# A decode kernel's five engine programs: emitted inside a block, or directly behind the common opening

## The chip, the cores and the metric

The kernel runs on one core of a Trainium2 chip. The metric is the device time of one execution in microseconds (us), lower being better. The core has five engines, each with a program of its own: PE (TensorE, matmuls), DVE (VectorE), ACT (ScalarE), POOL (GpSimd) and SP (SyncE, which here only issues transfers and waits for them). They meet through semaphores. Transfers run on 16 DMA engines.

## The reference

One decode step of a transformer block for a batch of 8 with one token each: sliding-window attention over cached keys and values, then a small MLP, each behind a layer norm.

```python
# x: 8 x 1 x 512; caches: 8 x 8 x 8192 x 128 bf16; 32 query heads, 8 kv heads
def _A_ref(x, k_cache, v_cache, wq, wo):
    W = min(4096, max(256, Sk // 4))              # 2048
    q = (x @ wq).reshape(B, Sq, Hq, Dh)           # transposed to b h q d
    k = repeat(k_cache[:, :, Sk - W:, :], rep)    # the last 2048 positions
    v = repeat(v_cache[:, :, Sk - W:, :], rep)
    scores = einsum("bhqd,bhkd->bhqk", q, k) * (Dh ** -0.5)
    p = softmax(scores)
    o = einsum("bhqk,bhkd->bhqd", p, v)
    return o.reshape(B, Sq, Hq * Dh) @ wo

def _B_ref(x, w1, w2, w3, w4):
    ...                                           # token shifts are all zero for S == 1
    x1 = x + hs
    return x1 + gelu(layernorm(x1) @ w3) @ w4

h  = x + _A_ref(layernorm(x), ...)
h2 = h + _B_ref(layernorm(h), ...)
```

## The kernel before

The kernel reads some 79 MB: for each of the 64 pairs of batch row and kv head 512 KB of keys and 512 KB of values, and the weights. SP issues all of these transfers on one queue (the helper `dma`, L181): first `wq`, then keys four heads at a time (`load_k`), values head by head (`load_v`), the slices of `wo` in between, and at the end `w3` and `w4`. PE transposes the keys (L277), ACT and DVE evict them (L285, L287), PE forms the scores (L299), the softmax runs per batch row in five steps, and the values are multiplied in (L359, L375). Behind the last pair come the output projection, the second layer norm and the MLP. The last steps are an addition on DVE (L598), a transposition on PE (L601), a copy to `out_sb` on DVE (L602), and SP's transfer of the 8 KB output (L605), behind which SP waits for `sem_out` in the function `store`.

The order on each engine is written out by hand. An object `Engine` collects the operations of one engine with the semaphore values that each waits for; nothing is emitted while they are collected. `Engine.emit` then writes the list to an engine: a wait where one is needed, the instruction, and an increment of the engine's own semaphore behind it. The kernel's last lines call `emit` for the five engines.

Ahead of all of this stands a common opening that the framework puts in when the program object is made (L628): POOL fills four constants, every engine drains, and the engines meet. Four engines report to POOL through one semaphore, and POOL releases them through another.

In the kernel before, the five calls of `emit` stand inside a `Block` (L609 to L614). A block gives each engine a section of its own. An unconditional branch leads each engine from the opening to its section, and another from the end of its section to a common end; at the end each engine drains, and the engines meet once more in the same way as in the opening. On SP the wait for `sem_out`, which has no instruction of its own behind it, rides on the branch to the end.

Of the kernel before, what the change touches and what calls it, by code (L numbers as in the profile page):

```python
# [67 lines left out]
def bass_sequential_preLN__sliding_block_cached__mixer_s_mlp__decode_kernel(  # L68
# [23 lines left out]
    with es:  # L92
# [84 lines left out]
        PE, AC, DV, PO, SP = (Engine(S(n)) for n in ("s_pe", "s_act", "s_dve", "s_pool", "s_sp"))  # L177
# [428 lines left out]
            e.wait_ge(sem_out, 16)  # L606
        SP.op(store, e_out, inc=False)

        with nc.Block() as block:  # L609
            block.gpsimd(PO.emit)  # L610
            block.sync(SP.emit)
            block.tensor(PE.emit)
            block.scalar(AC.emit)
            block.vector(DV.emit)  # L614


# [26 lines left out]
```

## Time and profile before

| | |
|---|---|
| median of three runs | 198.69 us (198.63 to 198.71) |
| span of the profiled execution, first to last instruction shown | 196.8 us |
| the profiled execution's own time | not listed; the median stands for it |
| between span and median | 1.9 us |
| transferred | 79.48 MB, mean 404 GB/s |
| PE, PEld, DVE, ACT, POOL busy | 149.0, 98.1, 83.1, 89.6, 7.7 us |

PE is TensorE's matmuls and PEld its weight loads. A name with a q behind it (SPq, PEq) is the engine's sequencer, which issues transfers and handles branches, drains and semaphores; such instructions are not counted as busy. A releaser, as in "<-DVE out_sb L602", is what ended the idle time before an instruction.

### The profile page before, as it was taken

What the parts mean: (1) busy time and instruction counts of PE and PEld (TensorE: products, weight loads), DVE (VectorE), ACT (ScalarE), POOL (GpSimd) and SP (SyncE); (2) the same over time, 40 slices, a digit from 0 to 9 for tenths busy, and PEclk for the clock granted to TensorE, in tenths of its full rate; (3) what the DMA queues carried; (4) which work ended last, traced back from release to release, by engine and by line L of the source; (5) the groups of instructions that cost most, each with busy time, mean ns of one, the idle gap of its engine ahead of it and who ended that gap; (6) DMA issues with size and microseconds to landing.
All of it is one profiled execution on the core that took longest, in us unless ns stands there. A gap on an engine that the chain in (4) does not pass through costs nothing.

```text
span 196.8 us, 4638 instructions
## 1 busy us (share of the span) xinstructions
PE 149.0 (76%) x2077; PEld 98.1 (50%) x2077; DVE 83.1 (42%) x182; ACT 89.6 (46%) x103; POOL 7.7 (4%) x16
## 2 busy tenths in 40 slices
PE   0037999999982989649992898669796989678854
PEld 0014666666640747237660656356554655235753
DVE  7502645446541346315451255416443544432231
ACT  3003766766751475424761365526652665420330
POOL 8300000000000000000000000000000000000030
PEclk9999999999999699966999699969997999965555
DMA  6999999999999999999999999999999999999991
GB/s 235 453 403 433 426 430 398 422 426 424 402 425 411 441 406 404 437 406 446 395 421 411 439 413 434 417 431 418 435 414 433 414 411 418 417 423 414 411 322 40
DMA packets 18276, 79.48 MB, mean 404 GB/s; under 512 B 1480, under 2 KB 7376, under 8 KB 16080
## 3 DMA queue, kind: packets, MB, share of 16 engines
q1 hardware_dynamic: 18240, 79.18, 98.0%
q8 instruction: 16, 0.26, 0.5%
q14 instruction: 4, 0.03, 0.0%
q10 hardware_dynamic: 16, 0.01, 0.0%
HBM read 79.18 MB, written 0.01 MB: 402 GB/s over the span
## 4 chain that ended last, share of the span: by engine, by line
DMA 70%; PE 22%; SPq 5%; DVE 1%; issue 1%; ACT 0%
DMA knat<-in_A_k_cache_dram 52%; PE kT_ps L277 13%; DMA vnat<-in_A_v_cache_dram 10%; DMA w_sb<-in_B_w_dram 9%; PE S_ps L299 6%; SPq L181 5%; PE o_rows L375 1%; PE o_rows L395 1%; PE sm L336 1%; PE S_ps L593 0%; DVE orow L385 0%; ACT orow L384 0%; PE o_rows L250 0%; PE sm L322 0%; PE sm L348 0%
## 5 line engine op out<-in xcount | busy, mean ns | idle before, releaser
L285 ACT ACTIVATE kT_sb<-kT_ps 128x1024 bf16<-128x1024 bf16 x64 | 65.4, 1024 | 61.2 <-PE kT_ps L277 61.2
L277 PE MATMUL kT_ps<-ident_b,knat 128*128 128x128 bf16 x1024 | 74.3, 231 | 21.8 <-DMA knat<-in_A_k_cache_dram 21.8
L277 PEld LDWEIGHTS kT_ps<-ident_b,knat 128*128 128x128 bf16 x1024 | 63.2, 104 | 46.2 <-DMA knat<-in_A_k_cache_dram 28.0
L287 DVE COPY kT_sb<-kT_ps 128x1024 bf16<-128x1024 bf16 x64 | 44.3, 694 | 59.0 <-PE kT_ps L277 59.0
L299 PE MATMUL S_ps<-kT_sb,qblk 128*32 128x512 bf16 x256 | 40.9, 612 | 0.0
L385 DVE TENSOR_TENSOR orow<-o_rows,orow 128x512 bf16<-128x512 f32 x14 | 9.7, 691 | 25.2 <-ACT orow L384 25.2
L375 PE MATMUL o_rows<-vnat,pT_sb 128*32 128x512 bf16 x224 | 15.6, 399 | 3.7 <-DMA vnat<-in_A_v_cache_dram 2.9
L384 ACT ACTIVATE orow<-o_rows 128x512 bf16<-128x512 f32 x14 | 8.6, 612 | 13.3 <-PE o_rows L375 13.2
L326 ACT ACTIVATE P_sb<-S_ps,negcol 128x512 bf16<-128x512 f32 x8 | 11.3, 1406 | 3.3 <-DVE negcol L325 3.3
L375 PEld LDWEIGHTS o_rows<-vnat,pT_sb 128*32 128x32 bf16 x224 | 6.2, 101 | 11.1 <-issue 8.3
L299 PEld LDWEIGHTS S_ps<-kT_sb,qblk 128*32 128x32 bf16 x256 | 7.2, 93 | 6.0 <-issue 1.2
L233 PE MATMUL S_ps<-wbig,xlnT 128*32 128x512 bf16 x32 | 3.6, 625 | 5.2 <-DMA wbig<-in_A_wq_dram 5.2
L581 POOL TENSOR_SCALAR r<-vsum 128x8 f32<-128x8 f32 x1 | 0.2, 243 | 182.8 <-DVE vsum L565 182.8
L395 PEld LDWEIGHTS o_rows<-sel,orow 128*128 128x128 bf16 x112 | 3.9, 101 | 5.8 <-issue 4.0
L239 ACT ACTIVATE qrow<-S_ps 128x512 bf16<-128x512 f32 x1 | 0.6, 597 | 12.2 <-PE S_ps L233 12.2
L216 PE MATMUL sm<-ident_b,xln_b 8*128 8x8 bf16 x4 | 0.3, 174 | 7.7 <-DVE xln_b L204 7.7
L308 DVE TENSOR_REDUCE mcol<-S_ps 128x1 f32<-128x512 f32 x8 | 5.5, 682 | 0.8 <-PE S_ps L299 0.8
L395 PE MATMUL o_rows<-sel,orow 128*128 128x4 bf16 x112 | 5.1, 167 | 0.6 <-DVE orow L385 0.6
L359 PEld LDWEIGHTS kT_ps<-pT_sb,vnat 128*128 128x128 bf16 x128 | 4.0, 105 | 2.6 <-issue 1.7
L233 PEld LDWEIGHTS S_ps<-wbig,xlnT 128*32 128x32 bf16 x32 | 1.3, 140 | 6.7 <-issue 6.7
L359 PE MATMUL kT_ps<-pT_sb,vnat 128*128 128x4 bf16 x128 | 4.5, 167 | 0.0
L322 PE MATMUL sm<-ones_f,negrow 1*128 1x1 f32 x16 | 3.0, 256 | 1.5 <-DVE negrow L318 1.5
(83 smaller groups left out, 83.6 us busy)
## 6 DMA issues: line engine op xcount, KB each, us to landing
knat<-in_A_k_cache_dram SPq DMA_DIRECT2D x16, 2048.0 KB, 19.4
vnat<-in_A_v_cache_dram SPq DMA_DIRECT2D x64, 512.0 KB, 18.6
wbig<-in_A_wq_dram SPq DMA_DIRECT2D x1, 4096.0 KB, 12.3
wbig<-in_A_wo_dram SPq DMA_DIRECT2D x4, 1024.0 KB, 20.3
w_sb<-in_B_w_dram SPq DMA_DIRECT2D x1, 1792.0 KB, 14.7
w_sb<-in_B_w_dram SPq DMA_DIRECT2D x1, 896.0 KB, 16.6
w_sb<-in_B_w_dram SPq DMA_DIRECT2D x1, 768.0 KB, 16.8
w_sb<-in_B_w_dram SPq DMA_DIRECT2D x1, 128.0 KB, 9.6
```

The source lines that it names most:

```text
L181: e.dma_start(dst, src).then_inc(sem, 16)
L277: ins = e.matmul(kT_ps[i % 2][:, n * 128:(n + 1) * 128], knat[:, i // KQ % NK, r * DH:(r + 1) * DH], ident_b[:, :], is_transpose=True)
L285: e_lo[i] = AC.op(lambda e: e.activation(kT_sb[:, i % NKT, 0:W // 2], kT_ps[i % 2][:, 0:W // 2], ACT.Copy), e_Tlo[i], e_QK.get(i - NKT))
L287: e_hi[i] = DV.op(lambda e: e.tensor_copy(kT_sb[:, i % NKT, W // 2:W], kT_ps[i % 2][:, W // 2:W]), e_Thi[i], e_QK.get(i - NKT))
L299: ins = e.matmul(S_ps[b % 2][32 * t:32 * (t + 1), :], qblk[:, b, g - g % KQ + t, at:at + H], kT_sb[:, i % NKT, :].rearrange("p (n t) -> p ...
L308: e_max[b] = DV.op(lambda e: e.tensor_reduce(mcol[:, :], S_ps[b % 2][:, :], AX.X, ALU.max), e_QK[G * b + G - 1], e_mT.get(b - 1))
L326: e_exp[b] = AC.op(lambda e: e.activation(P_sb[:, j, :].rearrange("p (c a w) -> p c w a", c=4, w=KQ), S_ps[j][:, :].rearrange("p (c w a) - ...
L359: ins = e.matmul(dst, vnat[:, i % NV, c * DH:(c + 1) * DH], pT_sb[:, b % 2, c, hq(g):hq(g) + R], start=(c == 0), stop=(c == NC - 1))
L375: ins = e.matmul(o_rows[32 * u:32 * (u + 1), :], pT_sb[:, b % 2, c, :], vnat[:, v0:v0 + KQ, c * DH:(c + 1) * DH], start=(c < 4), stop=(c > ...
L384: e = AC.op(lambda e: e.activation(orow[:, 0, :], o_rows[:, :], ACT.Copy), e_PV[i], e_oT.get(i - KQ))
L385: e_olo[i] = DV.op(lambda e: e.tensor_tensor(orow[:, 1, :], o_rows[:, :], orow[:, 0, :], ALU.subtract), e)
L395: ins = e.matmul(o_rows[:, R * t:R * (t + 1)], orow[:, part, t * DH:(t + 1) * DH], sel32[:, h:h + R], start=(part == 0), stop=(part == 1), ...
```

## The change

The block is gone. The five `emit` calls write straight behind the opening:

```diff
         SP.op(store, e_out, inc=False)
 
-        with nc.Block() as block:
-            block.gpsimd(PO.emit)
-            block.sync(SP.emit)
-            block.tensor(PE.emit)
-            block.scalar(AC.emit)
-            block.vector(DV.emit)
+        SP.emit(nc.sync)
+        AC.emit(nc.scalar)
+        PO.emit(nc.gpsimd)
+        DV.emit(nc.vector)
+        PE.emit(nc.tensor)
```

Each engine loses its two unconditional branches, its drain at the end and its part in the meeting at the end. On SP the wait for `sem_out` becomes a semaphore instruction of its own, the last of SP's program. The opening with its meeting stays. The operations of each engine, their order and their waits are the same; that the five lists are emitted in another order among themselves does not show, since each engine has its own program.

## The prediction

> **What bounds the kernel now.** I read the page first: the span, the DMA row, the rate and the chain that ended last.
>
> ```profile
> span 196.8 us, 4638 instructions
> DMA  6999999999999999999999999999999999999991
> GB/s 235 453 403 433 426 430 398 422 426 424 402 425 411 441 406 404 437 406 446 395 421 411 439 413 434 417 431 418 435 414 433 414 411 418 417 423 414 411 322 40
> ...
> q14 instruction: 4, 0.03, 0.0%
> ...
> DMA 70%; PE 22%; SPq 5%; DVE 1%; issue 1%; ACT 0%
> ```
>
> From the second slice to the last but one the DMA engines are busy at 9 tenths or more and move some 420 GB/s. The chain lies on DMA for 70% of the span. The body of the kernel, about 189 us of it, is a stream of keys, values and weights. The change touches no instruction of that body: engine by engine the two programs hold the same work in the same order, and only what stands ahead of the body and behind it differs. So I forecast no change between the first transfer and the store, and look at the two ends.
>
> The end first. The timeline of the last microseconds, and then the waits of SP's queue (us in total, times, longest):
>
> ```profile
> 194.12 0.22 DVE L598 TENSOR_TENSOR fT<-fin,S_ps 128x32 bf16<-128x32 f32 x1 [1.42 <-PE S_ps L593]
> 194.73 0.21 DVE L602 COPY out_sb<-sm 32x128 bf16<-32x128 bf16 x1 [0.38 <-PE sm L601]
> 194.97 0.37 SPq L605 DMA_DIRECT2D out_dram<-out_sb  x1
> ```
>
> ```profile
> SPq L605 <- DVE out_sb L602: 9.3, 1, 9.3
> SPq L609 <- DMA out_dram<-out_sb: 1.0, 1, 1.0
> SPq L609 <- PEq L609: 0.2, 1, 0.2
> ```
>
> DVE writes the output rows at 194.73, SP issues the store at 194.97, the issue takes 0.37, SP then waits 1.0 for the data to land, and it waits 0.2 more in something that has the line number of the block, L609. Up to the landing (194.97 + 0.37 + 1.0 = 196.34, about 196.4) everything is needed in the changed kernel too. What follows is the block's end. The view of that line lists all of it (duration ns min/median/max, first and last start):
>
> ```profile
> L609 POOLq EVENT_SEMAPHORE  x2: 17/17/17, 196.6 to 196.7; - x2
> L609 POOLq DRAIN  x1: 1782/1782/1782, 190.5 to 190.5; - x1
> L609 ACTq DRAIN  x1: 957/957/957, 191.3 to 191.3; - x1
> L609 PEldq DRAIN  x1: 342/342/342, 194.4 to 194.4; - x1
> L609 DVEq DRAIN  x1: 251/251/251, 194.7 to 194.7; - x1
> L609 SPq COMPARE_BRANCH  x1: 33/33/33, 196.4 to 196.4; - x1
> L609 SPq DRAIN  x1: 13/13/13, 196.5 to 196.5; - x1
> L609 SPq EVENT_SEMAPHORE  x1: 17/17/17, 196.7 to 196.7; - x1
> L609 ACTq EVENT_SEMAPHORE  x1: 17/17/17, 196.7 to 196.7; - x1
> L609 DVEq EVENT_SEMAPHORE  x1: 21/21/21, 196.7 to 196.7; - x1
> L609 PEldq EVENT_SEMAPHORE  x1: 51/51/51, 196.7 to 196.7; - x1
> ```
>
> Read it as a sequence. SP's branch holds the wait for the store and goes through at 196.4. SP drains at 196.5. POOL, the gatherer, sees the fourth arrival at 196.6 and releases the rest, and all leave at 196.7. Then the span ends, at 196.8. Two window rows show what runs meanwhile (busy us per engine, then granted clock, DMA share, GB/s):
>
> ```profile
> 194.97:196.38 1.41, 0.00 (x0) 0.00 (x0) 0.00 (x0) 0.00 (x0) 0.00 (x0) 0.50 0.03 6
> 196.38:196.80 0.42, 0.00 (x0) 0.00 (x0) 0.00 (x0) 0.00 (x0) 0.00 (x0) 0.50 0.05 20
> ```
>
> No engine computes in either, so the 0.42 us of the second row are bare.
>
> **The change part by part.**
>
> *Front branches.* The program before has one unconditional branch on each engine ahead of its work. The chain's first pieces (start, us) show what SP's costs:
>
> ```profile
> 0.66 0.07 issue
> 0.73 0.41 SPq L181
> 1.14 0.06 issue
> 1.19 16.63 DMA knat<-in_A_k_cache_dram
> ```
>
> Between the opening barrier and SP's first transfer, where the branch stands, lie 0.07 us. Between that transfer and the next, where no branch stands, lie 0.06. The branch is worth 0.01 at most, and no view has an instruction on lines 610 to 614. I take 0, with 0 and 0.01 as ends. The other engines start into waits that end far later than 0.7, so theirs are worth nothing. [...]
>
> *Drains of POOL, ACT, PE and DVE.* They take 1.78, 0.96, 0.34 and 0.25 us, but begin at 190.5, 191.3, 194.4 and 194.7. The last ends by 195.0, and the store's landing at 196.4 covers all of them: 0. Without that cover the longest remaining excess would be DVE's 0.25.
>
> *SP's branch, drain and the end barrier.* The conditional branch becomes a plain wait of the same semaphore as SP's last instruction: 17 ns (SP's EVENT_SEMAPHORE) in place of 33. Nothing of the kernel is queued behind it, and no engine waits for it. The way from the landing to the release then goes. It began at 196.4 (the branch, with 0.03 of its own) and ended with the span at 196.8: by the window row 0.42 us at most, and from it 0.02 for the wait that stays and what the rounded edges add. I take 0.35, from 0.30 to 0.40. This part lowers the span.
>
> *What comes behind the span.* The time is 198.69 us, the median of three runs (198.63 to 198.71), and the span 196.8. The own time of the profiled execution is not listed, so I set the sum against the median and carry the 1.9 us between the two as work without rows. If, as I take it, the engines meet once more in this remainder, then in the kernel before all five go into it together at 196.7, and the meeting ends with the slowest of them. In the changed kernel four of them reach it by 195.0 and only SP comes late. So a second gain is how much later than SP the slowest engine is on such a way. The nearest rows are those at the other end, where the engines come from the runtime's opening into the kernel:
>
> ```profile
> L628 SPq DRAIN  x1: 7/7/7, 0.0 to 0.0; - x1
> L628 DVEq DRAIN  x1: 10/10/10, 0.1 to 0.1; - x1
> L628 ACTq DRAIN  x1: 8/8/8, 0.1 to 0.1; - x1
> ...
> L628 PEldq DRAIN  x1: 8/8/8, 0.3 to 0.3; - x1
> ```
>
> SP is first, at 0.0, and PE last, at 0.3; DVE and ACT come at 0.1. PE's semaphore instruction in the list of L609 is also the slowest, 51 ns against 17. So PE is 0.2 behind the middle two and 0.3 behind SP. If SP's lead is its own speed, the second gain is 0.3; if SP was only let go first and is as fast as the others, 0.2; if engines need not meet at all, 0. It is not below 0, since SP's own steps behind the kernel stay the same. I take 0.25, with the ends 0 and 0.3.
>
> [...]
>
> **The sum.** Front 0, drains 0, end of block 0.35, later meeting 0.25: 0.60 us less. 198.69 - 0.60 = 198.09, say 198.1 us (0.30% less). A measurement of this kernel can tell about 0.2%, 0.4 us, from no change; its three runs lie within 0.08 us.
>
> **The rivals.**
>
> *Only SP's share (0.13).* Behind the span nothing waits for PE, or SP's own steps there are as long as PE's. Then the gain is the 0.35 alone: 198.69 - 0.35 = 198.34. For it: the 1.9 us have no rows. Against it: PE's 0.3 at the opening. By the bound of 0.2% this counts as no change.
>
> *Nothing (0.08).* The closing stretch has a start of its own that does not depend on the barrier. The window row from 196.38 has 20 GB/s for 0.42 us, 8 KB, when the store's own 8 KB (6 GB/s for 1.41 us) are through. The page's queue q14 has 4 loads of instructions, 0.03 MB, 8 KB each: this is one of them, code coming in just as the barrier runs. If SP's next steps lie in that code, SP waits for it in the changed kernel until about 196.7, and the time is 198.69 - 0.1 = 198.6. Against it: SP's DRAIN and EVENT_SEMAPHORE at 196.5 and 196.7 run while the load goes, so what SP does next was there already. A variant with the same result is that the runtime puts drains or a barrier of the same length there itself.
>
> *Slower (0.06).* The same load of code, but set off only when SP passes its last instruction. Now it has the barrier to hide under; without the barrier, and with every engine's program shorter, SP or PE could run into the closing code before it is loaded. The price is a transfer's whole way: the wait row of the store gives 1.0 us from issue to landing for 8 KB, with 0.37 of issue 1.4. The sum is 198.69 - 0.35 + 1.4 = 199.7, and with 1.0 it is 199.3. It decides if the load begins later than 0.35 us before SP needs its code. [...]
>
> **How the numbers follow.** Chances: forecast 0.73, SP's share only 0.13, nothing 0.08, slower 0.06. Predicted is the forecast's 198.1. Its own ends are 198.69 - 0.40 - 0.30 = 197.99 and, with 0.30 and 0.15, 198.24; another build's runs may lie as far off as the three of before among themselves, 0.08 us, on both sides, and I allow twice that. That gives 197.85 at the low end. The range reaches up over "SP's share only" (198.34, 0.30 to 0.40, the same scatter) to 198.5, and leaves out the two other cases, 0.14. Faster by over 0.2% is the forecast, 0.73; within 0.2% are the next two, 0.21; slower 0.06.
>
> **What would show it.** In the changed kernel's profile: no row for the block's end; the last instruction on SP a semaphore wait of some 17 ns at about 196.4; the span at 196.4, 0.35 to 0.4 shorter. The time falls by more than the span, so that what lies between them shrinks from 1.9 to about 1.65 us; if it stays at 1.9, the second term is wrong and the first rival right. If the span falls and the time does not, it is the second rival. SP's first transfer again begins 0.07 behind the opening barrier. The body (DMA row, store issued at about 195.0) stays where it is; a store issued more than 0.2 us earlier or later would mean that the body moved, which I have no reason for, and the forecast would then be right or wrong by chance.

## The result, and the profile after

The changed kernel takes 197.85 us (median; 197.59 to 198.05) against 198.66 of the kernel before. The ratio of the two is 0.9955, with a 95% interval from 0.9942 to 0.9968: 0.45% faster, 0.9 us. Forecast were 0.30% and 0.6 us. The ratio applied to the 198.69 of the forecast gives 197.80, just below the low end of the range, 197.85. The sign was forecast right, the size too small.

The page of the changed kernel, its span, its loads of code (queue q14, kind instruction: 4 packets, 0.03 MB, so some 8 KB each) and its chain:

```profile
span 196.3 us, 4627 instructions
...
q14 instruction: 4, 0.03, 0.0%
...
DMA 53%; PE 36%; SPq 3%; DVE 3%; ACT 3%; issue 1%
```

The span is 0.5 shorter, with 11 instructions fewer: five drains and six semaphore instructions of the meeting, while SP's branch has become a wait. The chain shows a trap: it lies 53% on DMA, where the kernel before had 70%, although nothing of the body changed. A second profile of the changed kernel, from the first experiment, has 70% again, and a third, from the last but one, 61%. So the share on DMA differs from one execution to the next and says nothing of the change.

The end, as timeline, as waits of SP's queue, and as the view of the last line (L606 is the wait for the store):

```profile
194.01 0.22 DVE L598 TENSOR_TENSOR fT<-fin,S_ps 128x32 bf16<-128x32 f32 x1 [1.28 <-PE S_ps L593]
194.62 0.21 DVE L602 COPY out_sb<-sm 32x128 bf16<-32x128 bf16 x1 [0.38 <-PE sm L601]
194.86 0.36 SPq L605 DMA_DIRECT2D out_dram<-out_sb  x1
```

```profile
SPq L605 <- DVE out_sb L602: 9.3, 1, 9.3
SPq L606 <- DMA out_dram<-out_sb: 1.0, 1, 1.0
```

```profile
L606 SPq EVENT_SEMAPHORE  x1: 17/17/17, 196.3 to 196.3; - x1
```

The body ends 0.11 earlier in this execution (store issued at 194.86, before at 194.97). From the store's issue to the landing it is the same 0.36 and 1.0. Then the kernel before had another 0.4 us, and here there are 17 ns.

The front, from the chain's first pieces:

```profile
0.66 0.07 issue
0.72 0.40 SPq L181
1.12 0.06 issue
1.18 16.54 DMA knat<-in_A_k_cache_dram
```

The 0.07 that held SP's branch is still 0.07: the branch cost nothing that these rows show.

### The profile page after: what moved, and what is told of

The parts are those of the page before. It is cut to its first block, busy times and chain, and to the rows that moved or that the text cites. A ratio compares the mean times of both kernels' runs of the same rounds, so it can differ in the third digit from the quotient of the medians.

```text
span 196.3 us, 4627 instructions
## 1 busy us (share of the span) xinstructions
PE 149.8 (76%) x2077; PEld 98.8 (50%) x2077; DVE 83.4 (42%) x182; ACT 89.6 (46%) x103; POOL 7.7 (4%) x16
## 4 chain that ended last, share of the span: by engine, by line
DMA 53%; PE 36%; SPq 3%; DVE 3%; ACT 3%; issue 1%
DMA knat<-in_A_k_cache_dram 43%; PE kT_ps L277 16%; DMA vnat<-in_A_v_cache_dram 10%; PE S_ps L299 8%; SPq L181 3%; PE o_rows L375 3%; PE kT_ps L359 1%; PE kT_ps L427 1%; PE S_ps L593 1%; PE S_ps L454 1%; PE sm L336 1%; PE o_rows L395 1%; ACT P_sb L326 1%; DVE orow L385 1%; ACT L580 1%
## 5 line engine op out<-in xcount | busy, mean ns | idle before, releaser
L375 PE MATMUL o_rows<-vnat,pT_sb 128*32 128x512 bf16 x224 | 16.1, 408 | 2.5 <-DMA vnat<-in_A_v_cache_dram 1.7
L340 DVE COPY pT_sb<-sm 128x512 bf16<-128x512 bf16 x8 | 3.3, 417 | 2.3 <-PE sm L336 2.2
```

What stands on the lines that cost most here:

```text
L375: ins = e.matmul(o_rows[32 * u:32 * (u + 1), :], pT_sb[:, b % 2, c, :], vnat[:, v0:v0 + KQ, c * DH:(c + 1) * DH], start=(c < 4), stop=(c > ...
```

## The experiments

Each execution gives a time and a span. Their difference, below called the rest, is the part without rows, in which the second term of the sum lies. It varies by 0.1 to 0.2 within one kernel, part of which is that spans are listed to a tenth, while the span varies by 0.3 and more. So the rest, averaged over several executions, is the sharper measure for what happens behind the kernel. The experiments ran on four chips, and each time the kernel before ran beside them: its median was 198.59 to 198.75 and its rest 1.82 to 1.84. All kernels but those of the last three experiments are the changed kernel with one edit.

**The changed kernel again.** 

> The changed kernel once more, beside the kernel before, to have time and span of each execution of both. Theory A (the engines meet once more behind the kernel, and in the kernel before a slow engine's own way there is what that meeting waits for): time minus span stays near 1.3 us in every execution of this kernel and near 1.9 in every one of the kernel before, and all scatter lies in the span. Theory B (the second part of the gain is an accident of the transfers in those four executions): time minus span overlaps between the two kernels.

Measured: 197.98 us, ratio 0.9957 (0.9942 to 0.9972). The rest is 1.37 on average (1.30 to 1.47 in four executions, after 1.31 in the first four); in 24 executions of the kernel before it is 1.82 (1.75 to 1.92). The two do not overlap. The medians of the spans are 196.55 and 196.90. So the gain has two parts: 0.35 in the span and 0.45 to 0.51 in the rest. The second is clear of the scatter; the first rests on four executions, and a later set of eight, below, has less.

**The meeting without the block.**

```diff
         PE.emit(nc.tensor)
+        nc.all_engine_barrier()
```

> The changed kernel with one meeting of all five engines (drains and semaphores) put behind the five programs, but without a block and its branches. If the meeting is all that the change took away: span near 196.8, time minus span near 1.9, time near 198.66, as the kernel before. If branches had a part of the gain: the time lies between 197.85 and 198.66, nearer to the first the larger their part.

Measured: 198.60 us, ratio 0.999 (0.9981 to 1.0), rest 1.80. The kernel before is back, though no branch is. The view of the line that holds the meeting reads as the block's end did:

```profile
L614 SPq DRAIN  x1: 7/7/7, 196.6 to 196.6; - x1
L614 SPq EVENT_SEMAPHORE  x1: 17/17/17, 196.8 to 196.8; - x1
...
L614 PEldq EVENT_SEMAPHORE  x1: 51/51/51, 196.8 to 196.8; - x1
```

The meeting has all of the gain that these runs can tell; a part of the branches, if there is one, is 0.15 us by the medians and under 0.4 by the interval, and neither the rest nor a row shows one.

**One engine late, and all four.** In each of these kernels one more engine, or all four, waits for the store as SP does, with no meeting:

```diff
+        PE.op(lambda e: e.wait_ge(sem_out, 16), inc=False)
         SP.emit(nc.sync)
```

PE: 

> The changed kernel, but PE too waits at its end for the store to land, so that PE and SP leave together; no meeting. As the prediction has it (PE has the slowest way to the meeting): the span stays near 196.4, time minus span goes from 1.3 back up by 0.3 to 0.6, to 1.6 to 1.9. If another engine is the slow one: up by less than 0.3. If no engine's lateness matters behind the kernel: 1.3 as it was.

All four: 

> The changed kernel, but PE, ACT, POOL and DVE all wait at their ends for the store to land, each by itself: the five leave together as behind the barrier, but without drains, gathering and release. Theory A (lateness of the slowest engine): span near 196.4, time minus span up to about 1.9, time some 0.35 below the kernel before, about 198.3. The rival (the drains and the semaphore traffic of the barrier cost the second part): time minus span stays near 1.3, time 197.9.

POOL: 

> The changed kernel, but POOL alone also waits at its end for the store to land. With PE alone late the time minus span rose from 1.3 to 1.6, with all four to 1.89; so another engine is slower than PE. Theory A' (POOL is that engine: at the end of the kernel before it is the one that gathers and releases, and its drain of 1.78 us is the longest): time minus span 1.85 to 1.9, as with all four, time about 198.45. Rival (it is DVE or ACT, or the four add up): 1.3 to 1.6.

ACT: 

> The changed kernel, but ACT alone also waits at its end for the store to land. Theory A' (POOL the slowest, the meeting goes by the slowest alone): ACT lies at or below PE, time minus span 1.35 to 1.6, time about 198.1. If the four engines' lateness adds up: about 0.15 above the changed kernel's 1.34 like any other. If ACT is the slowest: 1.85 to 1.9.

DVE: 

> The changed kernel, but DVE alone also waits at its end for the store to land. Theory A' (POOL slowest): DVE below POOL, time minus span 1.4 to 1.75, time about 198.2. If DVE is the slowest: 1.85 to 1.9. If the four add up (PE 0.25 of 0.55): about 0.1 above 1.34.

The added wait takes 51 ns on PE and 17 on POOL, at the time at which SP's ends:

```profile
L609 PEldq EVENT_SEMAPHORE  x1: 51/51/51, 196.6 to 196.6; - x1
```

```profile
L609 POOLq EVENT_SEMAPHORE  x1: 17/17/17, 196.7 to 196.7; - x1
```

So the span does not grow by it, and the rest shows the price:

| late beside SP | rest, mean (range) | more than the changed kernel's 1.33 | time |
|---|---|---|---|
| none (16 executions) | 1.33 (1.28 to 1.47) | | 197.85 to 198.05 |
| ACT | 1.48 (1.43 to 1.57) | 0.14 | 198.15 |
| PE | 1.61 (1.55 to 1.69) | 0.27 | 198.35 |
| POOL | 1.89 (1.84 to 1.96) | 0.55 | 198.39 |
| DVE | 1.94 (1.88 to 2.03) | 0.60 | 198.40 |
| all four | 1.89 (1.84 to 2.03) | 0.56 | 198.53 |
| kernel before | 1.82 (1.75 to 1.92) | 0.49 | 198.75 |

The four prices sum to 1.56, but all four together cost 0.56, as much as POOL or DVE alone. So the prices don't add up: by these numbers the latest counts. That is what a further meeting behind the kernel would do, with ways to it of different length; no row shows such a meeting, so that it is one is inferred. The table also refutes the idea that the drains and semaphores of the barrier make the rest longer: in the kernel with all four late there are none, and the rest is no shorter than that of the kernel before. The time itself is a weaker witness: with all four late 198.3 was expected, and 198.53 came, at a ratio of 0.9996 (0.9978 to 1.0014) to the kernel before, so that 0.35 for the missing meeting can't be read from it.

The slow engines are POOL and DVE, not PE, whose 0.27 is less than the 0.3 that its expectation set. POOL alone accounts for the kernel before. In the profiled execution of that kernel POOL's last instruction ends 0.09 ahead of the span, which ends with PE; with all four late it is 0.04, with POOL alone late 0.01. Counted from POOL's last instruction, the rest is 1.82 + 0.09 = 1.91 in the kernel before, 1.89 in the one with the meeting but no block, 1.93 with all four late and 1.89 with POOL alone late: nearly one number in four kernels.

DVE's 0.60 does not carry over. In the kernel before, DVE's last instruction ends 0.03 ahead of the span, so that its way is 1.85 there at most; with all four late it is 1.92 by the same count, and with DVE alone late 1.94. The page with DVE late shows something else that moved:

```profile
q14 instruction: 3, 0.02, 0.0%
```

The other kernels have four loads of code in this row. In the two kernels with DVE late the trace has the fourth behind the span, at 197.4, which is 1.1 us behind DVE's wait. Whether DVE's price is its own way or partly this load stays open; "DVE is the slowest", the rival in its row, is not settled. POOL's price has no such doubt, since with POOL late all four loads lie in the span.

**The meeting ahead of the store.** The kernel before, with its block, but with the store behind it:

```diff
-        SP.op(store, e_out, inc=False)
         with nc.Block() as block:
...
             block.vector(DV.emit)
+        store(nc.sync)
```

> The kernel before with its block and the meeting at its end, but the store and its wait moved behind the block, so that the five engines meet ahead of the store and SP alone is late at the very end. If what counts behind the span is only who comes late: time minus span 1.3 to 1.4 as in the changed kernel, although the meeting is there. The meeting then stands in SP's way ahead of the store, where it takes 0.3 to 0.45: span 196.8 to 197.0, time about 198.25, between the two kernels. If the meeting itself makes the closing stretch longer: time minus span 1.8.

Measured: 199.01 us, ratio 1.0014 (1.0003 to 1.0025), rest 1.37. The rest is as the theory says: with SP alone late at the very end, the block with its meeting did no harm behind the kernel here (1.37, as in the first repetition of the changed kernel). But the span is 197.6, not 196.8 to 197.0, and that neither side had foreseen. SP's waits show where it went:

```profile
SPq L608 <- PEq L608: 9.4, 1, 9.4
SPq L606 <- DMA out_dram<-out_sb: 1.9, 1, 1.9
```

The same 8 KB land 1.9 behind the issue, not 1.0. A window row over the store's packets (busy us of the five engines, clock, DMA share, GB/s):

```profile
196.60:196.90 0.30, 0.00 (x0) 0.00 (x0) 0.00 (x0) 0.00 (x0) 0.00 (x0) 0.50 0.22 53
```

53 GB/s for 0.30 us are 16 KB. The store has 8. The other 8 are one of the four loads of code of queue q14: the trace has its packet at 196.66. In the changed kernel the two lie side by side, 8 KB in each of two windows:

```profile
195.60:195.90 0.30, 0.00 (x0) 0.00 (x0) 0.00 (x0) 0.00 (x0) 0.00 (x0) 0.50 0.15 28
195.90:196.20 0.30, 0.00 (x0) 0.00 (x0) 0.00 (x0) 0.00 (x0) 0.00 (x0) 0.50 0.07 27
```

In the kernel before the load came later still, 0.4 behind the store's bytes, in the window from 196.38 that the prediction shows.

**The load of code moved away from the store.** Eight small memsets of an unused tile, on DVE, at the start, where DVE waits for POOL's iota until 1.34:

```diff
+        pad = sb([128, 8], dt.float32, "pad")
...
+        for n in range(8):
+            DV.op(lambda e, n=n: e.memset(pad[:, n:n + 1], 0.0), inc=False)
         e_idb = DV.op(lambda e: e.tensor_single_scalar(ident_b[:], iota_f[:], 0.0, ALU.is_equal), e_iota)
```

With the meeting ahead of the store: 

> The kernel with the meeting ahead of the store (block, then store), with the same eight memsets on DVE. Without them its span was 197.6 and SP waited 1.9 for the landing. Theory C (DVE's load of code meets the store): the wait falls to 1.0, the span to 196.8 to 197.0, the time to about 198.3; time minus span stays 1.37. Rival (the landing is late because four engines are in the closing stretch while the store is under way): 1.9 and 199.0 as before.

Measured: 198.09 us, ratio 0.9977 (0.9965 to 0.9989), rest 1.30, median span 196.8; the time is 0.2 below what was expected. The eight instructions take 0.9 us off by the times, and 0.7 by the two ratios, which allow for the two chips. SP's waits and the window rows over the store:

```profile
SPq L611 <- PEq L611: 9.4, 1, 9.4
SPq L609 <- DMA out_dram<-out_sb: 1.0, 1, 1.0
```

```profile
195.90:196.20 0.30, 0.00 (x0) 0.00 (x0) 0.00 (x0) 0.00 (x0) 0.00 (x0) 0.50 0.02 3
196.20:196.60 0.40, 0.00 (x0) 0.00 (x0) 0.00 (x0) 0.00 (x0) 0.00 (x0) 0.50 0.11 18
```

3 GB/s for 0.30 and 18 for 0.40 us are 8 KB: the store is alone, and lands in 1.0. The load now begins at 192.2 in the trace. The edit adds instructions to DVE alone, and the wait added on DVE had moved the same load the other way, to 197.4, while waits on PE, POOL and ACT left it at 196.0 to 196.6. So the runs point to DVE's code as what was loaded into the store's way, though no row names the engine whose code it is. That the two meet in time, and that the landing is late then, is shown. The last bytes of the store come behind the load: in the kernel without memsets the load's packet runs from 196.66 to 197.04, and the store's last 0.5 KB moves behind it, in this row:

```profile
196.90:197.60 0.70, 0.00 (x0) 0.00 (x0) 0.00 (x0) 0.00 (x0) 0.00 (x0) 0.50 0.00 1
```

Why they come behind it is not shown: that the two share a DMA engine there is the author's assumption, and the trace names no engine.

In the changed kernel, and that kernel beside it: 

> The changed kernel with eight small memsets of an unused tile on DVE at its start, where DVE waits for the iota until 1.34. They cost nothing there and shift DVE's later instructions by eight places in its program, so that DVE's last load of code, which in the changed kernel begins about 0.1 us behind the store's packets, should come some microseconds earlier. Theory C (that load, when it meets the store on its DMA engine, makes the landing late): no landing of the store above 1.1 us, the spans' upper tail gone, median the same as the changed kernel's or up to 0.1 below, 197.85 to 197.95. Rival (the load has nothing to do with the landing): median and scatter as the changed kernel's. Slower than 198.0 only if the eight instructions cost something.

> The changed kernel itself in more rounds, for its ratio to the kernel before and as the measure for the kernel with eight memsets. By the runs so far: time 197.85 to 198.0, time minus span 1.3 to 1.37, ratio 0.996.

Measured: 197.84 us with the memsets (197.59 to 198.21), ratio 0.9962 (0.9951 to 0.9974); 198.05 without (197.65 to 199.05), ratio 0.9968 (0.9956 to 0.9980); rests 1.35 and 1.33. The difference of the medians, 0.2, is within the scatter. With the load 4 us away, at 192.1, the rest is the same, so the load plays no part in the rest here. In the eight executions of the changed kernel the gain is 0.32% only: the rest is shorter by 0.49 as ever, but the median span by 0.05 (196.75 against 196.80). One cause of that is seen. The profiled execution of the kernel without memsets was a long one, of span 197.7; its wait for the store and the window row over the store:

```profile
SPq L606 <- DMA out_dram<-out_sb: 2.3, 1, 2.3
```

```profile
195.90:196.20 0.30, 0.00 (x0) 0.00 (x0) 0.00 (x0) 0.00 (x0) 0.00 (x0) 0.50 0.25 53
```

Again 16 KB in 0.30 us. So the changed kernel has the load of code so near to the store, 0.1 behind it in the first profile, that in one profiled execution they meet. (The profiled execution with ACT late, too, had a span of 197.6 and a wait of 2.3 for the landing.) By the packets in the trace, the store's bytes held up are half of the delay: their end comes 1.3 behind the end of the issue, at 196.75, in place of 0.7, and the landing 1.0 behind that in place of 0.4. For the second half no row shows a cause.

With the memsets no span of five executions was above 196.8; without, four of eight were. That is too few to say that the memsets end the tail: the kernel with the meeting ahead of the store and the memsets has four of ten spans above 196.8, up to 197.4. The spans between 196.9 and 197.2 have no profile, and what made them longer is not known.

**The opening meeting.** If a meeting costs what stands behind it, the opening one should cost the stream of transfers its start. The kernel with the memsets, with one instruction moved in the finished program: SP's first transfer goes ahead of SP's drain in the opening.

```diff
         PE.emit(nc.tensor)
+        ins = list(nc.cur_bb.bb.instructions)
+        sp = [i for i in ins if str(i.engine).endswith("SP")]
+        meet = [i for i in sp if type(i).__name__ in ("InstDrain", "InstEventSemaphore")][:2]
+        first = next(i for i in sp if "DMA" in type(i).__name__)
+        ins.remove(first)
+        ins.insert(ins.index(meet[0]), first)
+        nc.cur_bb.bb.instructions = ins
```

> The kernel with eight memsets on DVE, and SP's first transfer (wq) issued ahead of SP's part in the opening meeting instead of behind it. If a meeting costs what the engine behind it can't start, as at the end: the first transfer begins at 0.0 to 0.1 instead of 0.72, the stream of transfers and all that follows up to the store comes 0.5 to 0.7 us earlier, span 195.8 to 196.0, time minus span 1.35, time 197.2 to 197.35. The meeting itself ends later by SP's issue of 0.4 at most, which DVE, ACT and POOL have room for, since wq lands at 12. Rival 1: the stream is held by the slots that PE sets free and takes the lead back, time 197.84 as without. Rival 2: SP's drain behind an issued transfer waits for its data, 12 us, and the time grows by more than 5.

Measured: 197.18 us (197.08 to 197.81), ratio 0.9925 (0.9905 to 0.9945), median span 195.85, rest 1.34. The timeline's first row of SP, its next transfers, and the store:

```profile
0.00 0.41 SPq L182 DMA_DIRECT2D wbig<-in_A_wq_dram  x1
...
0.82 1.92 SPq L182 DMA_DIRECT2D knat<-in_A_k_cache_dram  x3
```

```profile
194.38 0.37 SPq L608 DMA_DIRECT2D out_dram<-out_sb  x1
```

SP's drain now stands behind that transfer. It takes 126 ns there, where it took 7 at 0.0, and ends before the next transfer:

```profile
L637 SPq DRAIN  x1: 126/126/126, 0.5 to 0.5; - x1
```

With the memsets alone the store was issued at

```profile
195.05 0.36 SPq L608 DMA_DIRECT2D out_dram<-out_sb  x1
```

so of the 0.73 us of lead at the front 0.67 arrive at the end in these two executions; the medians of the spans differ by 0.65, of the times by 0.66. The first rival fails: the slots don't take the lead back. The second fails too: the next transfers begin at 0.82, and the first one's data take 12.3 to land, as the page's row of it says (KB each, us to landing):

```profile
wbig<-in_A_wq_dram SPq DMA_DIRECT2D x1, 4096.0 KB, 12.3
```

So the drain on SP did not wait for the transfer's data. This version beats the kernel before by 0.75%, and its median is 0.67 to 0.87 below those of the changed kernel.

## Why the prediction was wrong in size

- *The body doesn't change.* Right. The store's issue moved by 0.11 in the profiled executions, which is within the scatter of a single kernel.
- *Front branches, 0.* Right on SP, whose rows show it: 0.07 before and after.
- *Drains of the four engines, 0.* Right as far as the kernel with all four late goes: it has no drains, and gained nothing behind the span by that.
- *Branch, drain and end barrier on SP, 0.35.* Right by the rows: the kernel before goes on for 0.4 behind the landing, the changed one for the forecast 17 ns of L606. The medians of the spans differ by 196.90 - 196.55 = 0.35 in the first experiment, but by 0.05 in the later eight executions, of which one at least had a late landing.
- *What comes behind the span, 0.25, with ends 0 and 0.3.* This is the step that failed. It measured 0.45 to 0.51, beyond its upper end. That the engines meet there was the author's assumption, and no row shows a meeting. What it implies fits the rest of every kernel here: 1.33 with SP alone late, 1.89 with all four late too, as if the end waited for the engine that is latest behind the span. The size came from the wrong rows. The order in which the engines come into the kernel (PE 0.3 behind SP, DVE and ACT 0.1) was taken for their order on the way out. On the way out PE costs 0.27 more than SP, which is near to the 0.3; but POOL and DVE, which are early at the opening, cost 0.55 and 0.60. POOL's first row at the opening, which the prediction left out, is as early as DVE's:

```profile
L628 POOLq INC_SWDGE_SEM  x1: 27/27/27, 0.1 to 0.1; - x1
```

So the order at the opening told nothing here of the order at the end. POOL's way alone gives the term: 1.89 from its last instruction, less the 0.09 by which that precedes the end of the span, less 1.33, is 0.47. The bound ought to have been wider: nothing in the trace excluded up to the whole 1.9 us without rows. The other end was too narrow as well: with its own lower end of 0 for this term the forecast reached up to 198.39, and the 0.15 that gave 198.24 has no row.

- *The sum.* With the measured terms it is 0.35 + 0.49 = 0.84, against 0.81 by the medians of the first comparison and 0.89 by its ratio. No third term is needed there. That the later eight executions gained 0.32%, close to the forecast 0.30%, is luck: the second term was as large as before, and longer spans took a part of the gain back.
- *Only SP's share.* Refuted: the rest shrank from 1.82 to 1.33, and no execution of the one kernel comes near those of the other.
- *Nothing.* Refuted by the same numbers. The 8 KB in the window from 196.38 were a load of code, as the text had it, but by the runs above DVE's rather than SP's, and the rest is the same, 1.35 against 1.33, when that load comes 4 us earlier.
- *Slower.* It did not happen by way of waiting for code: the span fell to 196.55 and the rest to 1.33. But the same load has another effect that no case had: where it meets the store in the changed kernel, as in one profiled execution, the landing takes 2.3 in place of 1.0, which is more than the whole gain. In the kernel before it came 0.4 behind the store's bytes, under the meeting; in the changed kernel it comes 0.1 behind them or upon them.

The tests named ahead gave the answers: the block's end has no rows, the wait is the last instruction at 196.3, and the time fell by more than the span. The rest fell further than named there, to 1.33 and not to 1.65.

## What to carry to other kernels

The meeting of all engines at the end cost twice here: its own rows, 0.4 us, and then 0.49 us of the rest, which is taken to be the slowest engine's way behind the kernel, begun only at the release. So let the engine that costs least when late be the last, here SP (one more engine late beside it cost 0.14 to 0.60 more), and put no meeting behind it. For a part of the time that no view shows, the difference of time and span, averaged over several executions, was steady here (1.82 to 1.84 for the kernel before on four chips), and making one engine late at a time ranked what is in it. Check then whether the edit moved anything else, as the wait on DVE moved a load of code. And look at both ends: the opening meeting here cost the first transfer 0.66 us, not much less than the 0.81 that the closing one cost the end.

## What the runs showed of the hardware that was not expected

- Behind the kernel the engines cost different times: late by the same wait beside SP, ACT cost 0.14, PE 0.27, POOL 0.55 and DVE 0.60 us more than SP alone, and all four together 0.56. With DVE late, a load of code also moved behind the span, to 197.4.
- Where an 8 KB load of code fell on the 8 KB store, the store landed 1.9 us behind its issue's end (the kernel with the meeting ahead of the store) and 2.3 us (the changed kernel, one profiled execution) in place of 1.0. Eight instructions more on DVE moved the load away, to 192.2, and took 0.9 us off one kernel (199.01 to 198.09, on two chips; 0.7 by the ratios).
- SP's drain behind an issued transfer of 4 MB took 126 ns, and the following transfer began at 0.82, while the data of the first took 12.3 to land: the drain did not wait for the data.
